# First batch of an attention and mixture-of-experts kernel: z's first group, v's maxima, constant matmuls and routing constants put elsewhere

## The chip, the cores and the metric

The kernel runs on one core of one Trainium2 chip. The metric is the device time of one execution in microseconds (us). TensorE, VectorE, ScalarE, GpSimd and SyncE are written PE, DVE, ACT, POOL and SP, as in the profile's rows. All DMAs of interest are issued on SP's queue.

## The reference

```
u, v: (8, 3072, 256)   z: (8, 3072, 64)   S = 3072
attn = max(z z^T / S, 0) ** 2
x    = (u * (attn v)).reshape(24576, 256)
logits = x w_gate ; expert = argmax(logits) ; gate = softmax(logits)[expert]
each of 8 experts takes its first 768 tokens, in order
out[token] = gate * relu(x w1[e]) w2[e] for kept tokens, 0 for the others
```

With 768 places for each of 8 experts, only the first tokens matter: the kernel computes attention for NB0 = 14 blocks of 512 query rows, checks on the chip that every expert is full, and runs the experts.

## The kernel before, in words

Every fp32 operand is split into two fp16 planes, "hi" and "lo", after a scaling by a power of two that comes from the largest absolute value (over partitions by an all-reduce on POOL). A block's attention runs over 12 pairs of key tiles of 128 (`attention`, line 723). For each pair PE makes the scores of both tiles (`sc`, line 772), ACT takes relu and square (lines 780, 784), DVE splits the square into hi and lo (`hl`, lines 788, 797), and PE multiplies with v's planes into four accumulators (`acc`, lines 872, 874: for each of 4 row tiles c and 2 key tiles one matmul of 512 columns and one of 256). Because attn is symmetric, strips of a block's squares are kept in DRAM (`kept`, line 809) and loaded turned by later blocks (`ld`, line 750). In block 1, pairs 0 and 1 come from such loads (pairs 12 and 13 of the whole sequence), and half of pair 15 comes from the core itself: line 803 sends two turning DMAs from `hl` into `corner`, and PE needs both at the first matmul of pair 15.

The first batch is prepared in `prepare(bt, True)` (line 315). z comes in three loads (line 337), then w_gate (`load_gate`, line 154), then v in six loads of 4 key tiles (line 343). Row norms of z (350, 354) give its maximum and, through POOL, its scale (`zb`). z is split and turned in six groups (`z_group`, line 375): hi on ACT (381), two DVE instructions (384, 385), eight transposes on PE into one PSUM tile `ztp` of one bank (392), and two copies out of it, one plane each, on ACT and DVE (395). Group 0 runs at once, the others when the planner's gates open. v's six maxima are dealt to ACT (loads 0, 2, 4, line 435) and DVE (loads 1, 3, 5, line 73), then reduced (442), all-reduced and turned into the scale (`v_bits`, `vs`); then v is split in pieces of two key tiles (456 on ACT, 459 on DVE). Thirty matmuls with an all-ones operand (`warm_up`, line 145) run on PE while z is loaded.

The order of the instructions on each engine is written by a planner (lines 170 to 272) that keeps its own clock for each engine (`clk`) with a cost for each item. Work is held in chains with a rank; `weave` goes through them by rank and emits what fits. A chain can wait for a gate (a key in `done`). Its clocks are costs that stand in the code and no times of the chip; they decide the order alone. A DMA with rank above 0 is emitted only while the DMA clock is at most 1.2 ahead of PE's (`fits`, line 244); DMAs of rank 0 and less, and loads, go past that rule. `need` moves PE's clock on until a key is there. Costs on the DMA clock: 1.46 for a `keep` or the load of u, 1.8 for a load of a kept strip, 2.3 for one of the eight writes that initialise `disp` (line 289), 4.4 for the next batch's z (`zraw`).

`more_consts` and `prep_gate` (lines 134, 156) make what the routing needs. They are a chain of rank 4, due at 25.0. `init_disp` (line 277), made at pair 1 with the gate "consts", clears a tile `dinit` on POOL (283), marks it on DVE (286) and writes it out in eight DMAs. At the end of every block `need` asks for the keys of all eight writes (line 881) before the block's routing is set up.

Of the kernel before, what the change touches and what calls it, by code (L numbers as in the profile page):

```python
# [9 lines left out]
F32 = mybir.dt.float32  # L10
F16 = mybir.dt.float16
I32 = mybir.dt.int32
AF = mybir.ActivationFunctionType
ALU = mybir.AluOpType
AX = mybir.AxisListType
# [3 lines left out]
P = 128  # L19
BLK = 512  # L20
# [6 lines left out]
def attention_moe_kernel(ctx: ExitStack, tc: tile.TileContext, u, v, z, w_gate, w1, w2, out, cap):  # L27
# [28 lines left out]
    def ts(o, i, s1, op0, s2=None, op1=None):  # L56
        if op1 is None:
            nc.vector.tensor_scalar(out=o, in0=i, scalar1=s1, scalar2=None, op0=op0)
        else:
            nc.vector.tensor_scalar(out=o, in0=i, scalar1=s1, scalar2=s2, op0=op0, op1=op1)  # L60
# [11 lines left out]
    def absmax(o, i):  # L72
        nc.vector.tensor_reduce(out=o, in_=i, axis=AX.XY if len(i.shape) == 3 else AX.X, op=ALU.max,
                                apply_absolute_value=True)
# [69 lines left out]

    def warm_up(n):

        t = ps.tile([P, BLK], F32, tag="m", name="warm")
        for _ in range(n):
            nc.tensor.matmul(t, lhsT=ones, rhs=ones.unsqueeze(1).to_broadcast([P, BLK // P, P]), start=True, stop=True)

    wg = const.tile([P, DC, E], F32, name="wg")

    def load_gate():
        nc.sync.dma_start(out=wg, in_=w_gate.rearrange("(c p) e -> p c e", p=P))
# [25 lines left out]
    def op(eng, cost, dep=0.0):  # L180
        start = max(clk[eng], dep + HOP)
        if eng in ("SP", "XB"):
            start = max(clk["SP"], dep + HOP)
            clk["SP"] = start + (0.5 if eng == "SP" else max(1.2, 0.3 + cost))
            clk["DMA"] = max(clk["DMA"], start + 1.4) + cost
            return clk["DMA"] + 1.0
        clk[eng] = start + cost
        return clk[eng]
# [126 lines left out]
    def prepare(bt, first=False):  # L315
# [5 lines left out]
        else:  # L321
            zr = row(z, bt.b).rearrange("(t p) d -> p t d", p=P)
        w = JT // zparts
        sq = []
        bt.vraw = {}
        key = lambda *k: (bt.id,) + k

        def ld_z(i):
            def f():
                if i == 0:  # L330
                    bt.zraw = sb.tile([P, JT, DQ], F32, tag="zraw", name="zraw", bufs=1)
                    bt.vm = sm.tile([P, NV], F32, tag="vm", name="vm")
                    bt.n2 = sm.tile([P, JT], F32, tag="n2", name="n2")
                    bt.zz = sb.tile([P, 2, S], F16, tag="zz", name="zz")
                zt = bt.zraw.rearrange("p (t r) d -> p t (r d)", r=2) if first else bt.zraw
                k = zt.shape[1] // zparts
                nc.sync.dma_start(out=zt[:, i * k:(i + 1) * k], in_=zr[:, i * k:(i + 1) * k])
            return f

        def ld_v(i):  # L340
            def f():
                t = sb.tile([P, 4, D], F32, tag="raw", name="vraw", bufs=6)
                nc.sync.dma_start(out=t, in_=vr[:, 4 * i:4 * i + 4, :])  # L343
                bt.vraw[i] = t
            return f
# [29 lines left out]
        def z_group(g):  # L375
            sl = slice(4 * g, 4 * g + 4)
            st = Bag()

            def hi():
                st.zhl = sb.tile([P, 4, 3 * DQ], F16, tag="zhl", name="zhl", bufs=3)  # L380
                nc.scalar.activation(st.zhl[:, :, 0:DQ], bt.zraw[:, sl], AF.Copy, scale=bt.zs)

            def lo():
                nc.vector.tensor_copy(st.zhl[:, :, 2 * DQ:3 * DQ], st.zhl[:, :, 0:DQ])
                nc.vector.scalar_tensor_tensor(out=st.zhl[:, :, DQ:2 * DQ], in0=bt.zraw[:, sl], scalar=bt.zs,
                                               in1=st.zhl[:, :, 0:DQ], op0=ALU.mult, op1=ALU.subtract)

            def tr():
                st.tp = ps.tile([P, 2, 4, P], F16, tag="m", name="ztp")
                for k in range(4):  # L390
                    for r in range(2):
                        nc.tensor.transpose(st.tp[:, r, k, :], st.zhl[:, k, r * DQ:r * DQ + P], ident)

            def ev(r):
                return lambda: (nc.scalar.copy if r else nc.vector.tensor_copy)(  # L395
                    bt.zz[:, r, g * BLK:(g + 1) * BLK].rearrange("p (t q k) -> p t k q", t=2, k=2),
                    st.tp[:, r].rearrange("p (t k) q -> p t k q", k=2))

            return [[("ACT", 0.4, hi, None)], [("DVE", 0.53, lo, key("zl", g))], [("PE", 0.5, tr, None)],
                    [("ACT", 0.48, ev(1), key("ze", g)), ("DVE", 0.6, ev(0), key("z", g))]]  # L400

        ZW = 6
# [26 lines left out]
            return ("SP", 1.2, f, key("z", 0) if h else None)  # L429

        def v_abs(i):
            def f():
                if first and i % 2 == 0:
                    junk = sb.tile([P, 4, D], F32, tag="x", name="junk")
                    nc.scalar.activation(junk, bt.vraw[i], AF.Abs, accum_out=bt.vm[:, i:i + 1])
                else:
                    absmax(bt.vm[:, i:i + 1], bt.vraw[i])
            return ("ACT", 1.04, f, None) if first and i % 2 == 0 else ("DVE", 1.13, f, None)

        def v_red():  # L440
            bt.vmx = sm.tile([P, 1], F32, tag="vmx", name="vmx")
            nc.vector.tensor_reduce(out=bt.vmx, in_=bt.vm, axis=AX.X, op=ALU.max)

        def v_all():
            bt.vma = sm.tile([P, 1], F32, tag="vma", name="vma")
# [6 lines left out]
        def v_piece(t0, k):  # L452
            o, i, a = slice(t0, t0 + k), t0 // 4, t0 % 4

            def hi():
                nc.scalar.activation(bt.v2[:, o, 0, :], bt.vraw[i][:, a:a + k], AF.Copy, scale=bt.vs)

            def lo():
                nc.vector.scalar_tensor_tensor(out=bt.v2[:, o, 1, :], in0=bt.vraw[i][:, a:a + k], scalar=bt.vs,  # L459
                                               in1=bt.v2[:, o, 0, :], op0=ALU.mult, op1=ALU.subtract)  # L460
                for j in range(t0 + 2, t0 + k, 2):
                    done[key("v", j // 2)] = clk["DVE"]

            return [[("ACT", 0.19 + 0.21 * k, hi, None)], [("DVE", 0.06 + 0.285 * k, lo, key("v", t0 // 2))]]

        def factor():
            q = sm.tile([P, 1], F32, tag="cb0", name="cb0")
# [13 lines left out]

        if first:
            tz = [(ld_z(i)(), op("SP", 0.75))[1] for i in range(zparts)]
            load_gate()
            tv = [(ld_v(i)(), op("SP", 1.46))[1] for i in range(NV)]
        for i in range(zparts):
            st = [[("ACT", 1.4 / zparts, norm1(i), None)], [("DVE", 1.7 / zparts, norm2(i), key("n", i))]]
            if first:
                Chain(st, -3, tz[i])
            else:  # L490
                Chain([[("SP", 4.4, ld_z(i), None)]] + st, 1, slow=8.0)
        for i in range(NV):
            def mark(i=i):
                e, c, f, _ = v_abs(i)
                return e, c, f, key("m", i)
            if first:
                Chain([[mark()]], -2, tv[i], gate={1: key("zl", 0), 2: key("ze", 0), 3: key("z", 0)}.get(i))
            else:
                Chain([[("SP", 1.46, ld_v(i), None)], [mark()]], 2, slow=8.0)

# [12 lines left out]
        def v_rest():  # L513
            chain = [[("DVE", 0.1, v_red, None)], [("POOL", 0.4, v_all, None)], [("DVE", 0.6, v_bits, key("vs"))]]
            if first:
                def pieces():
                    for i in range(JT // 2):
                        Chain(v_piece(2 * i, 2), -2, done[key("vs")], gate=("pair", i - 2) if i > 1 else None)
                chain.append([("PE", 0.0, pieces, None)])
            else:  # L520
                chain += pipe([v_piece(t, 4) for t in range(0, JT, 4)])
            Chain(chain, -2 if first else 2, need_max("m", NV))

        def need_max(k, n):
            return max(done[key(k, i)] for i in range(n))


        watchers.append((lambda: all(key("n", i) in done for i in range(zparts)), z_rest))
        watchers.append((lambda: all(key("m", i) in done for i in range(NV)), v_rest))
        watchers.append((lambda: key("s") in done and key("v", 0) in done and "gate" in done,  # L530
                         lambda: Chain([[("DVE", 0.4, factor, key("f"))]], 3, max(done[key("v", 0)], done["gate"]))))
        bt.key = key
# [190 lines left out]
    def attention(blocks, hook):  # L723
# [31 lines left out]
        def loads_to(p):  # L755
            while loads and loads[0] <= p:
                load(loads.popleft())
# [65 lines left out]
        def scores_to(k):  # L823
            while ahead[0] < len(computed) and computed[ahead[0]] < k:
                scores(*divmod(computed[ahead[0]], 2))
                ahead[0] += 1
# [14 lines left out]
                  -2, clk["PE"])  # L841

        loads_to(1)
        scores_to(4)
        for p in range(NP):
            n, g = divmod(p, NPAIR)
            bt, ib, c0, cc = blocks[n]
# [244 lines left out]
    with tc.manual_schedule():  # L1092
# [12 lines left out]
        prepare(b0, True)  # L1105
        make_consts()
        warm_up(30)
        Chain([[("DVE", 1.2, more_consts, "consts")], [("DVE", 0.8, prep_gate, "gate")]], 4, 25.0)

        def put_zeros(i):  # L1110
            def f():
# [105 lines left out]
```

## Time and profile before

| | us |
|---|---|
| median of three runs (lowest, highest) | 807.35 (807.35, 810.51) |
| profiled execution, its own time | 808.55 |
| its span, first to last instruction | 806.7 |
| PE busy | 781.0 (97%) |
| DVE, ACT, POOL busy | 536.7, 434.3, 130.2 |

Numbers in the views are us from the span's start; a stretch is written 0:30. A row of a timeline gives start, length, engine, line, operation, what is written and read, a count, and in brackets the idle time before it with what ended it. "xN" on a row merges N neighbours. PEclk is the granted clock of PE as a share of full speed: 1.00 is 2.4 GHz and 0.50 is 1.2 GHz.

### The profile page before, as it was taken

Reading aid. Unit: us, or ns where it says so; the run is one execution under the profiler, and the core shown is the slowest. Engines: PE = TensorE matmul, PEld = TensorE weight load, DVE = VectorE, ACT = ScalarE, POOL = GpSimd, SP = SyncE. Lnnn points to the kernel's source line nnn. Section 1 sums busy time; section 2 is a strip of 40 time slices with the busy share of each in tenths; the row PEclk is TensorE's granted clock in tenths of the full one; section 3 lists DMA queues with packets and bytes.
Section 4 is the critical chain, followed back from the end, with each engine's and each line's share of the span. In section 5 each row is a group of like instructions: output and inputs, shape, how many; then the busy total and the mean of one; then the engine's idle time right before and its main releaser. Section 6 shows DMA issues by size and latency. Waiting matters only on the chain.

```text
span 806.7 us, 13434 instructions
## 1 busy us (share of the span) xinstructions
PE 781.0 (97%) x4964; PEld 460.7 (57%) x4964; DVE 536.7 (67%) x1186; ACT 434.3 (54%) x748; POOL 130.2 (16%) x123
## 2 busy tenths in 40 slices
PE   6999999999999999999999999999799999999996
PEld 2555555555655555555556655565566666666663
DVE  6886887863536889976454359888674675665741
ACT  5786746461405767763524148674564564554541
POOL 0000121110202010202112020203211313303202
PEclk8799999999999999999999999999999999999999
DMA  6399998969897996949597969972797847655001
GB/s 195 131 339 253 309 256 205 262 173 226 187 202 154 305 281 168 277 129 269 136 270 172 202 153 297 272 188 78 183 323 291 260 137 285 217 164 173 27 14 44
DMA packets 278736, 165.48 MB, mean 205 GB/s; under 512 B 218125, under 2 KB 244058, under 8 KB 278656
## 3 DMA queue, kind: packets, MB, share of 16 engines
q1 hardware_dynamic: 273760, 151.69, 71.3%
q0 software_dynamic: 4896, 12.79, 4.7%
q8 instruction: 42, 0.69, 0.4%
q14 instruction: 38, 0.31, 0.1%
HBM read 35.86 MB, written 77.75 MB: 141 GB/s over the span
## 4 chain that ended last, share of the span: by engine, by line
PE 87%; DMA 5%; DVE 3%; SPq 2%; ACT 2%; issue 1%; POOL 0%; POOLq 0%; ACTq 0%
PE acc L872 32%; PE acc L874 16%; PE hps L1012 14%; PE sc L772 10%; PE yps L1033 10%; PE yps L1034 5%; DMA ld<-kept 2%; DMA vraw<-in_v 1%; DMA fxt<-disp 1%; DMA zz<-zhl 1%; SPq L584 1%; DVE hh L998 1%; PE lg L591 0%; SPq L343 0%; ACT r L780 0%
## 5 line engine op out<-in xcount | busy, mean ns | idle before, releaser
L872 PE MATMUL acc<-v,hl 128*128 128x512 f16 x760 | 257.7, 381 | 2.9 <-DVE v L459 2.9
L874 PE MATMUL acc<-v,hl 128*128 128x256 f16 x760 | 208.2, 274 | 0.0
L780 ACT ACTIVATE r<-sc 128x512 f32<-128x512 f32 (+1 forms) x212 | 116.1, 551 | 140.3 <-PE sc L772 133.4
L872 PE MATMUL acc<-v,ld 128*128 128x512 f16 x488 | 162.4, 379 | 3.4 <-DMA ld<-kept 2.0
L874 PE MATMUL acc<-v,ld 128*128 128x256 f16 x488 | 133.0, 272 | 0.0
L1012 PE MATMUL hps<-fxt,wt 128*128 128x384 f16 (+2 forms) x816 | 127.2, 316 | 4.0 <-DVE hh L998 1.8
L1033 PE MATMUL yps<-wt,hh 128*128 128x512 f16 x384 | 125.5, 379 | 0.0
L872 PEld LDWEIGHTS <-hl 128*128 128x128 f16 x760 | 74.7, 98 | 88.4 <-issue 1.9
L772 PE MATMUL sc<-zz 128*128 128x512 f16 (+1 forms) x424 | 118.6, 364 | 3.6 <-DVE zz L395 2.3
L797 DVE TENSOR_TENSOR hl<-a,hl 128x1024 f16<-128x1024 f32 (+1 forms) x106 | 118.2, 1115 | 3.5
L84 POOL DMA_INDIRECT disp<-xr,slot x54 | 67.6, 1252 | 300.0 <-ACT a L784 147.7
L1012 PEld LDWEIGHTS <-wt 128*128 128x128 f16 x816 | 76.0, 98 | 54.1 <-issue 5.1
L1034 PE MATMUL yps<-wt,hh 128*128 128x256 f16 x384 | 104.7, 273 | 0.4 <-DVE hh L998 0.4
L788 DVE CAST hl<-a 128x1024 f16<-128x1024 f32 (+1 forms) x106 | 67.9, 640 | 54.9 <-ACT a L784 47.7
L784 ACT ACTIVATE a<-r 128x1024 f32<-128x1024 f32 (+1 forms) x106 | 102.6, 968 | 3.2
L998 DVE SCALAR_TENSOR_TENSOR hh<-hps,hh 128x384 f16<-128x384 f32 (+2 forms) x136 | 70.7, 530 | 39.2 <-ACT hh L997 38.8
L997 ACT ACTIVATE hh<-hps 128x384 f16<-128x384 f32 (+2 forms) x136 | 62.9, 471 | 49.6 <-PE hps L1012 49.0
L874 PEld LDWEIGHTS <-hl 128*128 128x128 f16 x760 | 74.7, 98 | 24.2 <-issue 2.2
L872 PEld LDWEIGHTS <-ld 128*128 128x128 f16 x488 | 47.7, 98 | 56.9 <-DMA ld<-kept 3.3
L84 POOL DMA_INDIRECT out<-ys,sid x48 | 55.2, 1150 | 124.3 <-DVE ys L1043 86.1
L1033 PEld LDWEIGHTS <-hh 128*128 128x128 f16 x384 | 37.5, 98 | 44.1
L1040 ACT ACTIVATE ys<-yps,sg 128x256 f32<-128x256 f32 x48 | 22.8, 475 | 74.1 <-PE yps L1034 67.1
(134 smaller groups left out, 685.1 us busy)
## 6 DMA issues: line engine op xcount, KB each, us to landing
kept<-hl SPq DMA_DIRECT2D x62, 512.0 KB
out<-zero SPq DMA_DIRECT2D x48, 512.0 KB
wraw<-in_moe_w SPq DMA_DIRECT2D x32, 512.0 KB
vraw<-in_v SPq DMA_DIRECT2D x18, 512.0 KB
u<-in_u SPq DMA_DIRECT2D x13, 512.0 KB
disp<-dinit SPq DMA_DIRECT2D x8, 792.0 KB
zraw<-in_z SPq DMA_DIRECT2D x2, 768.0 KB
zz<-zz SPq DMA_DIRECT2D x4, 384.0 KB
```

The lines of the kernel that those rows point to most:

```text
L84: r = nc.gpsimd.indirect_dma_start(out=dst, out_offset=bass.IndirectOffsetOnAxis(ap=idx, axis=0), in_=src, in_offset=None, bounds_check=bo ...
L772: nc.tensor.matmul(s[:, 0:w], lhsT=bt.zz[:, 0, j * P:(j + 1) * P], rhs=bt.zz[:, r, q0:q0 + w], start=(r == 0), stop=(r == 1))
L780: nc.scalar.activation(sct[p][:, jj, :], s[:, 0:w], AF.Relu)
L784: nc.scalar.activation(sq[p], sct.pop(p), AF.Square)
L788: nc.vector.tensor_copy(hl[:, :, :, 0, :], sq[p].rearrange("p j (t k) -> p j t k", k=HB))
L797: nc.vector.tensor_sub(hl[:, :, :, 1, :], a.rearrange("p j (t k) -> p j t k", k=HB), hl[:, :, :, 0, :])
L872: nc.tensor.matmul(o, lhsT=a(0, jj, c), rhs=bt.v2[:, j], start=(j == 0), stop=False, skip_group_check=True)
L874: nc.tensor.matmul(o[:, 0, :], lhsT=a(1, jj, c), rhs=bt.v2[:, j, 0, :], start=False, stop=(j == JT - 1), skip_group_check=True)
L998: [("DVE", 0.07 + w * 0.00104, lambda: nc.vector.scalar_tensor_tensor(out=tl, in0=src, scalar=0.0, in1=th, op0=ALU.max, op1=ALU.subtract), ...
L1012: nc.tensor.matmul(o, lhsT=wx.w1[:, d, wp, f * P:(f + 1) * P], rhs=sx.xt[:, xp * DC + d, a:a + w], start=(q == 0), stop=(q == len(seq) - 1))
L1033: nc.tensor.matmul(y, lhsT=hid(0, f)[:, sl], rhs=w, start=(f == 0), stop=False, skip_group_check=True)
L1034: nc.tensor.matmul(y[:, 0], lhsT=hid(1, f)[:, sl], rhs=w[:, 0], start=False, stop=(f == FC - 1), skip_group_check=True)
```

## The change

In the first batch: w_gate is loaded behind v. z's group 0 takes its hi plane on DVE, and all groups' transposes go into two PSUM tiles, one for each plane. v's maxima become seven: load 5 is split into halves, and ACT takes loads 0 and 2 and the second half of 5, DVE takes 1, 3, 4 and the first half of 5. `warm_up` charges PE's planner clock for each matmul, takes its tile from `acc`, and is called in five more places: 5 matmuls behind group 0's transposes, 9 behind those of groups 1 and 2, 5 behind the scores of the first pair and 10 behind those of the second. v's first piece is split into its two key tiles, of rank -3. The chain with `more_consts` and `prep_gate` is due at 45.0.

```diff
     def warm_up(n):
-        t = ps.tile([P, BLK], F32, tag="m", name="warm")
+        t = ps.tile([P, BLK], F32, tag="acc", name="warm", bufs=4)
         for _ in range(n):
+            op("PE", 0.2155)
             nc.tensor.matmul(t, lhsT=ones, ...)
...
+        NM = NV + 1 if first else NV
...
             def hi():                                   # z_group
...
+                if g == 0:
+                    ts(st.zhl[:, :, 0:DQ], bt.zraw[:, sl], bt.zs, ALU.mult)
+                else:
+                    nc.scalar.activation(st.zhl[:, :, 0:DQ], bt.zraw[:, sl], AF.Copy, scale=bt.zs)
...
             def tr():
-                st.tp = ps.tile([P, 2, 4, P], F16, tag="m", name="ztp")
-                for k in range(4):
-                    for r in range(2):
-                        nc.tensor.transpose(st.tp[:, r, k, :], st.zhl[:, k, r * DQ:r * DQ + P], ident)
+                st.tp = [ps.tile([P, 4, P], F16, tag="m", name="ztp") for r in range(2)]
+                for r in range(2):
+                    for k in range(4):
+                        nc.tensor.transpose(st.tp[r][:, k, :], st.zhl[:, k, r * DQ:r * DQ + P], ident)
+                warm_up({0: 5, 1: 9, 2: 9}.get(g, 0))
...
-            return [[("ACT", 0.4, hi, None)], [("DVE", 0.53, lo, key("zl", g))], ...
+            return [[("ACT", 0.4, hi, None) if g else ("DVE", 0.3, hi, None)], [("DVE", 0.53, lo, key("zl", g))], ...
...
         def v_abs(i):
+            act = first and i in (0, 2, NV)
+            src = lambda: bt.vraw[min(i, NV - 1)][:, 2 * (i == NV):4 - 2 * (first and i == NV - 1)]
...
+            half = 0.5 if first and i >= NV - 1 else 1.0
+            return ("ACT", 1.04 * half, f, None) if act else ("DVE", 1.13 * half, f, None)
...
         if first:
             tz = [(ld_z(i)(), op("SP", 0.75))[1] for i in range(zparts)]
-            load_gate()
             tv = [(ld_v(i)(), op("SP", 1.46))[1] for i in range(NV)]
+            load_gate()
...
                 def pieces():
-                    for i in range(JT // 2):
+                    for t in (0, 1):
+                        Chain(v_piece(t, 1), -3, done[key("vs")])
+                    for i in range(1, JT // 2):
                         Chain(v_piece(2 * i, 2), -2, done[key("vs")], gate=("pair", i - 2) if i > 1 else None)
...
         loads_to(1)
+        scores_to(2)
+        if straight[0] and len(blocks) > 1:
+            warm_up(5)
         scores_to(4)
+        if straight[0] and len(blocks) > 1:
+            warm_up(10)
...
-        Chain([[("DVE", 1.2, more_consts, "consts")], [("DVE", 0.8, prep_gate, "gate")]], 4, 25.0)
+        Chain([[("DVE", 1.2, more_consts, "consts")], [("DVE", 0.8, prep_gate, "gate")]], 4, 45.0)
```

## Rows read from the trace of the kernel before

**Rows 1.** The page's busy times and instruction counts, PE, PEld, DVE, ACT and POOL with their shares of the span.
```profile
PE   781.0 (97%) x4964; PEld 460.7 (57%) x4964; DVE 536.7 (67%) x1186; ACT 434.3 (54%) x748; POOL 130.2 (16%) x123
```

**Rows 2.** The longest of PE's waits over the whole span: the instruction, whom it waited for, us in total, times, the longest.
```profile
PE acc L872 <- DVE v L459: 2.9, 1, 2.9
```

**Rows 3.** The windows view: for each stretch the busy time of PE, PEld, DVE, ACT and POOL with instruction counts, then PEclk, the DMA engines' share, GB/s.
```profile
12.00:13.00 1.00, 0.00 (x0) 0.00 (x0) 0.69 (x1) 1.00 (x2) 0.00 (x0) 0.88 1.11 351
...
29.50:30.00 0.50, 0.50 (x3) 0.29 (x2) 0.46 (x3) 0.50 (x2) 0.04 (x1) 0.67 0.17 33
```

**Rows 4.** The timeline of PE from 10 to 31.
```profile
10.91 0.61 PE L392 MATMUL ztp<-ident,zhl 128*128 128x128 f16 x8 [0.80 <-DVE zhl L385]
13.10 1.89 PE L772 MATMUL sc<-zz 128*128 128x512 f16 x4 [1.58 <-DVE zz L395]
...
21.00 0.59 PE L872 MATMUL acc<-v,hl 128*128 128x512 f16 x1 [2.87 <-DVE v L459]
...
26.15 1.89 PE L772 MATMUL sc<-zz 128*128 128x512 f16 x4 [0.73 <-DVE zz L395]
...
30.12 1.03 PE L772 MATMUL sc<-zz 128*128 128x512 f16 x4
```

**Rows 5.** The timeline of DVE from 12 to 30.
```profile
12.31 0.73 DVE L395 COPY zz<-ztp 128x512 f16<-128x512 f16 x1 [0.42 <-ACT zz L395]
...
15.85 1.22 DVE L73 TENSOR_REDUCE vm<-vraw 128x1 f32<-128x1024 f32 x1 [1.60 <-DMA vraw<-in_v]
17.18 0.16 DVE L442 TENSOR_REDUCE vmx<-vm 128x1 f32<-128x6 f32 x1
...
18.28 0.68 DVE L788 CAST hl<-a 128x1024 f16<-128x1024 f32 x1
19.00 1.23 DVE L797 TENSOR_TENSOR hl<-a,hl 128x1024 f16<-128x1024 f32 x1
20.19 2.07 DVE L459 SCALAR_TENSOR_TENSOR v<-vraw,vsr,v 128x512 f16<-128x512 f32 x3
...
26.84 0.27 DVE L58 TENSOR_SCALAR tri<-iota,part 128x128 f16<-128x128 f32 x1
...
28.78 0.78 DVE L58 TENSOR_SCALAR wg<-wg,wgsr 128x16 f16<-128x16 f32 x1
```

**Rows 6.** The timeline of ACT, z's group 0.
```profile
9.62 0.49 ACT L381 ACTIVATE zhl<-zraw,zb 128x256 f16<-128x256 f32 x1
```

**Rows 7.** The timeline of POOL.
```profile
17.44 0.36 POOL L77 PARTITION_ALL_REDUCE vma<-vmx  x1 [8.35 <-DVE vmx L442]
27.84 0.35 POOL L77 PARTITION_ALL_REDUCE wgma<-wgm  x1 [10.04 <-DVE wgm L73]
28.05 1.48 POOL L283 MEMSET dinit<- 128x1584 f32 x1
```

**Rows 8.** The windows view again (columns as in rows 3), while z, w_gate and v are loaded.
```profile
4.00:5.00 1.00, 1.00 (x4) 0.41 (x3) 0.48 (x1) 0.81 (x2) 0.00 (x0) 1.00 0.98 196
5.00:6.00 1.00, 1.00 (x4) 0.34 (x3) 0.87 (x2) 0.30 (x1) 0.00 (x0) 1.00 0.57 168
```

**Rows 9.** Groups of instructions from 0 to 31: line, engine, operation, out<-in, shapes, count, then busy us and mean ns of one, then idle time before them.
```profile
L354 DVE TENSOR_REDUCE n<-sq 128x8 f32<-128x512 f32 x3 | 2.1, 686 | 2.8 <-ACT sq L350 2.7
...
L385 DVE SCALAR_TENSOR_TENSOR zhl<-zraw,zb,zhl 128x256 f16<-128x256 f32 x3 | 1.4, 477 | 0.0
...
L58 DVE TENSOR_SCALAR ident<-iota,part 128x128 f16<-128x128 f32 x1 | 0.3, 286 | 0.0
```

**Rows 10.** The timeline of SP's DMA issues: the first of the eight writes of `disp`, and from the last `keep` of block 0 to the corner.
```profile
31.92 0.36 SPq L289 DMA_DIRECT2D disp<-dinit  x1
...
63.99 0.37 SPq L809 DMA_DIRECT2D kept<-hl  x1
64.42 1.62 SPq L289 DMA_DIRECT2D disp<-dinit  x2
66.14 1.15 SPq L337 DMA_DIRECT2D zraw<-in_z  x1
74.56 3.31 SPq L803 DMA_TRANSPOSE corner<-hl  x2
```

**Rows 11.** The page's DMA issues: out<-in, queue, operation, count, KB of each.
```profile
disp<-dinit SPq DMA_DIRECT2D x8, 792.0 KB
```

**Rows 12.** The DMA view of the stretches 68:70 and 72:74: packets, MB, mean rate, and how many packets were small.
```profile
DMA packets 128, 0.71 MB, mean 355 GB/s; under 512 B 16, under 2 KB 16, under 8 KB 128
...
DMA packets 2014, 0.52 MB, mean 258 GB/s; under 512 B 2014, under 2 KB 2014, under 8 KB 2014
```

**Rows 13.** The windows view (columns as in rows 3) around the corner's DMAs.
```profile
54.00:62.00 8.00, 8.00 (x48) 4.57 (x47) 5.53 (x7) 6.78 (x9) 0.00 (x0) 1.00 1.05 274
...
66.00:70.00 4.00, 4.00 (x25) 2.24 (x24) 2.33 (x6) 3.09 (x7) 0.00 (x0) 1.00 1.06 385
...
71.50:75.00 3.50, 3.50 (x23) 2.12 (x22) 3.33 (x11) 2.15 (x5) 0.00 (x0) 1.00 1.18 224
75.00:75.80 0.80, 0.80 (x6) 0.39 (x5) 0.76 (x2) 0.80 (x3) 0.00 (x0) 1.00 0.13 28
...
77.80:78.60 0.80, 0.80 (x6) 0.49 (x5) 0.77 (x2) 0.45 (x1) 0.00 (x0) 1.00 0.81 164
```

**Rows 14.** The timeline of PE, the corner's first use.
```profile
78.72 0.38 PE L872 MATMUL acc<-v,corner 128*128 128x512 f16 x1
```

More of the change, by code (lines that the diff above doesn't have):

```diff
@@ L331, in f @@
                     bt.zraw = sb.tile([P, JT, DQ], F32, tag="zraw", name="zraw", bufs=1)
-                    bt.vm = sm.tile([P, NV], F32, tag="vm", name="vm")
+                    bt.vm = sm.tile([P, NV + 1], F32, tag="vm", name="vm")
                     bt.n2 = sm.tile([P, JT], F32, tag="n2", name="n2")
@@ L380, in hi @@
                 st.zhl = sb.tile([P, 4, 3 * DQ], F16, tag="zhl", name="zhl", bufs=3)
-                nc.scalar.activation(st.zhl[:, :, 0:DQ], bt.zraw[:, sl], AF.Copy, scale=bt.zs)
+                if g == 0:
+                    ts(st.zhl[:, :, 0:DQ], bt.zraw[:, sl], bt.zs, ALU.mult)
+                else:
+                    nc.scalar.activation(st.zhl[:, :, 0:DQ], bt.zraw[:, sl], AF.Copy, scale=bt.zs)
             def lo():
@@ L396, in ev @@
                     bt.zz[:, r, g * BLK:(g + 1) * BLK].rearrange("p (t q k) -> p t k q", t=2, k=2),
-                    st.tp[:, r].rearrange("p (t k) q -> p t k q", k=2))
-            return [[("ACT", 0.4, hi, None)], [("DVE", 0.53, lo, key("zl", g))], [("PE", 0.5, tr, None)],
+                    st.tp[r].rearrange("p (t k) q -> p t k q", k=2))
+            return [[("ACT", 0.4, hi, None) if g else ("DVE", 0.3, hi, None)], [("DVE", 0.53, lo, key("zl", g))], [("PE", 0.5, tr, None)],
                     [("ACT", 0.48, ev(1), key("ze", g)), ("DVE", 0.6, ev(0), key("z", g))]]
@@ L431, in v_abs @@
         def v_abs(i):
+            act = first and i in (0, 2, NV)
+            src = lambda: bt.vraw[min(i, NV - 1)][:, 2 * (i == NV):4 - 2 * (first and i == NV - 1)]
             def f():
-                if first and i % 2 == 0:
+                if act:
                     junk = sb.tile([P, 4, D], F32, tag="x", name="junk")
-                    nc.scalar.activation(junk, bt.vraw[i], AF.Abs, accum_out=bt.vm[:, i:i + 1])
-                else:
-                    absmax(bt.vm[:, i:i + 1], bt.vraw[i])
-            return ("ACT", 1.04, f, None) if first and i % 2 == 0 else ("DVE", 1.13, f, None)
+                    n = src().shape[1]
+                    nc.scalar.activation(junk[:, 0:n], src(), AF.Abs, accum_out=bt.vm[:, i:i + 1])
+                else:
+                    absmax(bt.vm[:, i:i + 1], src())
+            half = 0.5 if first and i >= NV - 1 else 1.0
+            return ("ACT", 1.04 * half, f, None) if act else ("DVE", 1.13 * half, f, None)
         def v_red():
             bt.vmx = sm.tile([P, 1], F32, tag="vmx", name="vmx")
-            nc.vector.tensor_reduce(out=bt.vmx, in_=bt.vm, axis=AX.X, op=ALU.max)
+            nc.vector.tensor_reduce(out=bt.vmx, in_=bt.vm[:, 0:NM], axis=AX.X, op=ALU.max)
         def v_all():
@@ L462, in lo @@
                     done[key("v", j // 2)] = clk["DVE"]
-            return [[("ACT", 0.19 + 0.21 * k, hi, None)], [("DVE", 0.06 + 0.285 * k, lo, key("v", t0 // 2))]]
+            return [[("ACT", 0.19 + 0.21 * k, hi, None)], [("DVE", 0.06 + 0.285 * k, lo, key("v", t0 // 2) if t0 + k > t0 // 2 * 2 + 1 else None)]]
         def factor():
@@ L483, in prepare @@
             tz = [(ld_z(i)(), op("SP", 0.75))[1] for i in range(zparts)]
+            tv = [(ld_v(i)(), op("SP", 1.46))[1] for i in range(NV)]
             load_gate()
-            tv = [(ld_v(i)(), op("SP", 1.46))[1] for i in range(NV)]
         for i in range(zparts):
@@ L491, in prepare @@
                 Chain([[("SP", 4.4, ld_z(i), None)]] + st, 1, slow=8.0)
-        for i in range(NV):
+        for i in range(NM):
             def mark(i=i):
@@ L496, in prepare @@
             if first:
-                Chain([[mark()]], -2, tv[i], gate={1: key("zl", 0), 2: key("ze", 0), 3: key("z", 0)}.get(i))
+                Chain([[mark()]], -2, tv[min(i, NV - 1)], gate={1: key("zl", 0), 2: key("ze", 0), 3: key("z", 0)}.get(i))
             else:
@@ L521, in v_rest @@
                 chain += pipe([v_piece(t, 4) for t in range(0, JT, 4)])
-            Chain(chain, -2 if first else 2, need_max("m", NV))
+            Chain(chain, -2 if first else 2, need_max("m", NM))
         def need_max(k, n):
@@ L528, in prepare @@
         watchers.append((lambda: all(key("n", i) in done for i in range(zparts)), z_rest))
-        watchers.append((lambda: all(key("m", i) in done for i in range(NV)), v_rest))
+        watchers.append((lambda: all(key("m", i) in done for i in range(NM)), v_rest))
         watchers.append((lambda: key("s") in done and key("v", 0) in done and "gate" in done,
```

## The prediction

> **What bounds the kernel now.** I read the page's busy times first: PE is busy for 781.0 of 806.7 us [rows 1], so a change in one stage is worth what it moves PE there. PE's waits come next: the longest one of all is the first `acc` matmul, which waits 2.9 us for v's first piece [rows 2]. From 30 us on PE hardly pauses, so the first batch's preparation costs its own length, and a later stall of PE costs its own length too. Third come the timelines of PE and DVE between 10 and 31: the reader is to see three gaps on PE, before the first scores at 13.10, before the first `acc` at 21.00 and before the scores at 26.15, and the next pair's scores at 30.12 [rows 4]. I use 30.12 as the mark for the front: everything of pair 0 is done there. The windows view shows the clock: it falls to 1.2 GHz within 12:13, after the warm-up matmuls end at 10.1 and eight transposes and a gap follow, and comes back to 2.4 GHz within 29.5:30, after PE has worked without a gap from 26.15 [rows 3, 4]. Last I follow SP's queue to the end of block 0, because the change moves eight large DMAs on it [rows 10].
>
> A measurement of this kernel tells about 0.5% (4 us) from no change.
>
> **The front, part by part.**
>
> *w_gate behind v.* Its small packets hold up the DMA engines: 196 and 168 GB/s in 4:5 and 5:6, against 351 later [rows 3, 8]. That is (155 + 183)/351, about 1.0 us of DMA time. Between 0 and 1.0 I take 0.9: the last of v lands at 14.95 in place of 15.85 [rows 5].
>
> *z's group 0.* On DVE hi costs between 0.29 (half as long a row, from fp32 to fp16 with a pointer) and the 0.49 that ACT takes [rows 6, 9]; the hop between engines goes. With two banks DVE's copy doesn't wait for ACT's: it started at 12.31, 0.42 late and 0.73 long [rows 5]. So scores start about 1 us before 13.10. I cost all this at nothing for the end: v's maximum is late behind it (15.85). Were v no longer late, this 1 us would count.
>
> *v's maxima.* Load 5's DVE half takes 0.69 in place of 1.22 [rows 5, 9]; ACT's half lies beside it. Without anything else the reduction `vmx` would move from 17.18 to about 15.7.
>
> *The order turns round.* The planner's clock now counts the warm-up matmuls: 30 bring PE to 6.67, the transposes and 5 more to 11.34, two scores, 5, two scores and 10 to 16.30, where pair 0 opens the gate of z's group 2. In that pass its hi and lo end at 15.75 on the planner's clocks; transposes are allowed 0.5 later, at 16.25, so they just fit, and its evictions follow. v's reduction chain is made only when a pass begins, so `vmx` comes behind group 2's two DVE instructions and its eviction. Before, group 2's DVE work stood behind v's first pieces. On the chip: both halves end at 15.65; ACT's hi 0.49 more, 16.15; from there to the transposes took 0.80 in group 0, 16.95; transposes 0.61, eviction 0.73, so `vmx` is at 18.3, 1.1 later than now [rows 4 to 6]. In the queue behind it are the scale, the first square's split and all of v's pieces.
>
> *The constants go, the clearing of `dinit` comes.* DVE loses 26.84 to about 29.8 [rows 5]; PE has none of these waits, so it gains nothing by itself. But `init_disp`'s clearing on POOL needs nothing from DVE. Emitted now before the gate's all-reduce, it stands right behind v's all-reduce. Before, it ended 1.69 after the start of the all-reduce in front of it [rows 7]; now that is 18.3 + 0.26 + 1.69 = 20.3. The row that shows a price: the gate's fp32-to-fp16 scaling of 16 elements took 0.78 beside that clearing and ended with it, where one of 128 elements took 0.29 alone [rows 5, 7, 9]. The first cast of `hl` would start 1.10 behind `vmx`, at 19.4 [rows 5]; between 0 and 0.9 I take 0.9, so 20.3. The Trainium skill (SBUF — State Buffer, section Who interferes with whom) speaks against the change here: a DVE cast or scaling in a two-port mode and a GpSimd instruction hold a shared pair of ports exclusively, and the later one blocks fully. By that rule the whole 0.9 is paid; without it the sum is 0.9 less. The trace has the one row that agrees.
>
> *First `acc`.* From cast to v's piece 1.91, a piece of one tile 0.48 [rows 5, 9]: 22.7, against 21.00, 1.7 later.
>
> *Warm-ups and pair 0.* The 38 new matmuls at 0.2155 cost nothing where PE waits. They hold the clock to about 19.6, when the nine behind group 2's transposes end. Then PE waits 3.1 us, longer than the 2.7 after which the clock fell within 12:13, so I take it as fallen again [rows 3, 4]. In exchange group 2 is done, and the gap before 26.15 shrinks. From 22.7: eight half-speed matmul pairs to 25.4, group 1's transposes, nine fillers, four scores, eight pairs: 30.5 if the clock comes back 3.7 us after 22.7 as it did after 26.15, 31.9 if later, 29.9 if it never fell. Against 30.12 I take **+0.6**, bounds -1.2 (no blocking, clock held) and +2.3.
>
> **The corner.** Constants due at 45 instead of 25 delay all eight writes of `disp`; the first is planned at 47.6 instead of 29. On the planner's DMA clock a write (2.3) goes only when that clock is within 1.2 of PE's; keeps, u and two strip loads go past it and fill it. Following the clocks pair by pair, write 0 goes in pair 5, write 1 at the end of pair 7, and then none until the last keep. The other six come out together, because block 0's end needs their keys. On SP they stand behind the last keep (63.99) and ahead of `zraw` and the corner's two turning DMAs. Now two stand there [rows 10].
>
> The queue is in order: `zraw` was issued at 66.14 to 67.29, yet its small packets are not in 68:70 (16) but in 72:74 (2014) [rows 10, 12]. The engines were full in 54:62 and until 75.0, then empty; the corner's second transfer ended at 78.6, and PE used it at 78.72 with no slack seen [rows 13, 14]. A write is 792 KB at 385 GB/s, 2.1 us [rows 11, 13]. Four more put the end of `zraw` at 75.0 + 8.4 = 83.4. The two transposes then follow at once, since SP issued them meanwhile: 0.8 each [rows 13], 85.0. PE comes in step with the front, so its shift cancels: at most 85.0 - 78.6 = 6.4. Idle time of the engines within 54 to 75 may swallow some. Bounds 3 and 8 (transposes as slow as now: 3.6 from 75.0 to 78.6), I take **+5.5**. A PE idle so long loses its clock by the same row: 3.7 us at half speed [rows 3, 4], between 0 and 1.8, I take **+1.8**. Nothing behind gives it back: PE is the bound.
>
> *Costed at nothing:* v's first piece in two halves (ACT half a tile ahead of DVE); the seventh column of `vm`; `warm`'s bank; the 2.6 us of constants put into DVE near 48, covered by squares prepared three pairs ahead (without that cover up to 2.6).
>
> **Sum.** 0.6 + 5.5 + 1.8 = 7.9. On the profiled execution's 808.55 that is 816.45; it stands 1.2 above the median, so against 807.35 I predict **815.2**.
>
> **Rivals.**
> 1. *Not slower: the corner is in time.* If no more than two or three writes are left behind the last keep, or the engines had 5 us to spare, the queue ends near 77 and only the front counts: 807.35 + 0.6, about 808.0, from 806.1 to 809.7. For it: DMA is nearly free until 46. Against it: 54:62 is full [rows 13], and 78.6 to 78.72 leaves no slack. Deciding point: `zraw`'s packets end by 76. Chance 0.25.
> 2. *The corner's transposes take their 3.6 us after the queue has run dry, and the clock comes back late:* 8 + 1.8 + 2.3, 819.4. Chance 0.13.
> 3. *The front pays fully:* the clock holds from the warm-ups through pair 0, `vmx` near 15.7 because group 2 does not stand ahead of it, first `acc` near 19.5, pair 0 done at 26: -4.1, 803.2 with the corner in time. Against it is the order above. Chance 0.06.
> The forecast has 0.56, its own range 811 to 818.
>
> **How the numbers follow.** Slower by over 0.5%: forecast and rival 2, less a part that stays within 4 us, 0.65. Same: rival 1 and that part, 0.28. Faster: 0.07. The range 805.8 to 818.6 leaves out most of rival 3 and of rival 2.
>
> **What would show it.** On DVE `vmx` behind a copy of `zz`; a cast of `hl` that starts as `dinit`'s clearing ends; first `acc` at 22 to 23; two writes of `disp` ahead of block 0's last keep and six behind; a wait of PE on corner of 3 to 8 us near 78 with PEclk at 0.50 after it. If the writes stand otherwise, or PE doesn't wait there, the corner step is wrong; if `vmx` comes before 17, the order step is.

## The result and the profile after

The changed kernel takes 819.22 us (median; 817.51 to 821.08), the kernel before 807.85 beside it: ratio 1.0133, 95% interval 1.0107 to 1.0159. The forecast was 815.2, so the direction was right; the time lies 0.6 above the top of the range. The kernel before was 0.5 slower here than the 807.35 that the forecast started from: the ratio on 807.35 gives 818.1, just inside the range. In run 1 below, one of twelve executions took 1180.17 at a granted clock of 0.654; it counts in that run's median (808.24; 808.06 without it) and not in its ratio. The profiled execution took 819.1, with a span of 817.3 against 806.7: 10.6 us to explain, where the forecast had 7.9. One profile stands for one execution: the one of the kernel before took 808.55, 0.7 above its median.

Counting the 128x512 `acc` matmuls from the start in both timelines of PE, and comparing the starts of the same ones, gives a ledger of where PE falls behind:

| the n-th such matmul | before | after | behind | what lies between |
|---|---|---|---|---|
| 8th, end of pair 0 | 29.76 | 30.01 | 0.25 | the front |
| 105th | 71.79 | 75.50 | 3.71 | a wait for `relu` |
| 111th | 74.17 | 79.47 | 5.30 | half clock |
| 118th | 77.31 | 84.15 | 6.84 | logits, now ahead of it, and a wait for `xt` |
| 121st, first of the corner | 78.72 | 89.16 | 10.44 | a wait for the corner |
| 127th | 81.10 | 93.16 | 12.06 | half clock |
| 334th | 166.93 | 176.65 | 9.72 | part given back |

PE's waits of the changed kernel between 60 and 110 (us in total, times, longest). Before, the only one there was 1.3 for a drain.
```profile
PE acc L891 <- DMA corner<-hl: 3.4, 1, 3.4
PE sc L786 <- ACT r L794: 3.3, 1, 3.3
PE lg L605 <- DMA xt<-xr: 0.9, 1, 0.9
```
The windows view of the changed kernel (columns as in rows 3): two stretches at 1.2 GHz, each just after one of the long waits.
```profile
72.00:75.00 3.00, 0.00 (x0) 0.00 (x0) 2.15 (x11) 2.07 (x5) 0.00 (x0) 1.00 1.02 414
76.00:79.40 3.40, 3.40 (x12) 1.55 (x11) 2.95 (x4) 2.20 (x5) 0.00 (x0) 0.53 0.98 371
84.00:90.00 6.00, 2.52 (x17) 1.30 (x18) 3.62 (x10) 1.65 (x2) 0.00 (x0) 0.99 1.00 183
90.20:93.40 3.20, 3.20 (x11) 1.50 (x10) 0.00 (x0) 0.71 (x2) 0.00 (x0) 0.52 0.94 318
```
SP's queue after, to set beside [rows 10]. Two writes of `disp`, the last keeps, six writes, as forecast; but then `xt` and `zraw` go ahead of the corner, where before it was `zraw`, corner, `xt`.
```profile
48.81 0.34 SPq L290 DMA_DIRECT2D disp<-dinit  x1
...
54.38 0.46 SPq L290 DMA_DIRECT2D disp<-dinit  x1
...
63.31 1.30 SPq L823 DMA_DIRECT2D kept<-hl  x2
64.66 7.24 SPq L290 DMA_DIRECT2D disp<-dinit  x6
74.46 8.23 SPq L598 DMA_TRANSPOSE xt<-xr  x4
82.75 0.58 SPq L339 DMA_DIRECT2D zraw<-in_z  x1
83.42 4.80 SPq L817 DMA_TRANSPOSE corner<-hl  x2
```
ACT's timeline there. `relu` (L794), for which PE waits from 71.98 to 75.28, could have run at 69.2, when its scores were done, but stands behind the routing's casts (L587), and those wait for a chain of DVE.
```profile
68.76 0.37 ACT L853 COPY x<-acc 128x256 f32<-128x256 f32 x1 [0.28 <-PE acc L893]
72.69 0.91 ACT L587 ACTIVATE xr<-x,rsr 128x256 f16<-128x256 f32 x2 [3.56 <-DVE rsr L60]
73.84 0.91 ACT L587 ACTIVATE xr<-x,rsr 128x256 f16<-128x256 f32 x2 [0.24 <-DVE xr L653]
74.65 0.57 ACT L794 ACTIVATE r<-sc 128x512 f32<-128x512 f32 x1
```
Both inversions have one cause in the code, and runs 3 and 9 show it: putting PE's planned clock back takes both away, and moving that clock alone brings both. Line 900 asks for the keys of all eight writes (`need`), and `need` moves the planner's PE clock on by 0.1 until they are there. Followed through the planner's costs, that wait is 1.4 us before and 9.3 after (67.1 to 76.4), since the writes that are left pass one by one at 2.3 each. When it is over, the routing of block 0 seems long due and the next scores only just made, so the routing is put first on ACT and SP.

The front, to set beside [rows 4, 5, 7]: PE, then DVE, then POOL.
```profile
12.53 1.04 PE L786 MATMUL sc<-zz 128*128 128x512 f16 x4 [0.88 <-DVE zz L401]
...
18.72 2.10 PE L150 MATMUL warm<-ones 128*128 128x512 f16 x9
23.52 0.39 PE L891 MATMUL acc<-v,hl 128*128 128x512 f16 x1 [2.70 <-DVE v L471]
...
30.34 1.03 PE L786 MATMUL sc<-zz 128*128 128x512 f16 x4
```
```profile
18.69 0.73 DVE L401 COPY zz<-ztp 128x512 f16<-128x512 f16 x1 [0.57 <-PE ztp L397]
19.32 0.14 DVE L454 TENSOR_REDUCE vmx<-vm 128x1 f32<-128x7 f32 x1
...
20.39 1.42 DVE L802 CAST hl<-a 128x1024 f16<-128x1024 f32 x1
21.84 1.23 DVE L811 TENSOR_TENSOR hl<-a,hl 128x1024 f16<-128x1024 f32 x1
```
```profile
19.55 0.36 POOL L77 PARTITION_ALL_REDUCE vma<-vmx  x1 [11.14 <-DVE vmx L454]
19.78 1.49 POOL L284 MEMSET dinit<- 128x1584 f32 x1
```
The reduction `vmx` stands behind group 2's copy, the cast beside the clearing takes 1.42 instead of 0.68, and the first `acc` is 2.5 late; but it runs at full clock (0.39), and pair 0 ends 0.2 late.

### The profile page after: what moved, and what is told of

Its sections match the earlier page's. It is cut to its first block, busy times and chain, and to the rows that moved or that the text cites. A ratio compares the mean times of both kernels' runs of the same rounds, so it can differ in the third digit from the quotient of the medians.

```text
span 817.3 us, 13505 instructions
## 1 busy us (share of the span) xinstructions
PE 786.6 (96%) x5002; PEld 462.9 (57%) x5002; DVE 538.5 (66%) x1189; ACT 433.5 (53%) x748; POOL 129.1 (16%) x123
## 4 chain that ended last, share of the span: by engine, by line
PE 84%; DMA 7%; DVE 5%; ACT 2%; SPq 1%; issue 1%; POOL 0%; POOLq 0%; DVEq 0%; ACTq 0%
PE acc L891 30%; PE acc L893 15%; PE hps L1031 14%; PE yps L1052 10%; PE sc L786 9%; PE yps L1053 5%; DMA ld<-kept 2%; DMA vraw<-in_v 1%; DMA fxt<-disp 1%; DMA corner<-hl 1%; DVE hl L802 1%; DMA zz<-zhl 1%; DMA kept<-hl 1%; SPq L345 1%; DVE hh L1017 1%
## 5 line engine op out<-in xcount | busy, mean ns | idle before, releaser
L794 ACT ACTIVATE r<-sc 128x512 f32<-128x512 f32 (+1 forms) x212 | 115.6, 551 | 146.5 <-PE sc L786 137.9
L1059 ACT ACTIVATE ys<-yps,sg 128x256 f32<-128x256 f32 x48 | 22.7, 474 | 74.8 <-PE yps L1053 67.8
```

What stands on the lines that cost most here:

```text
L794: nc.scalar.activation(sct[p][:, jj, :], s[:, 0:w], AF.Relu)
```

## The experiments

All times are medians; "of before" is the ratio to the kernel before with its 95% interval. In what follows, order means that ACT's and SP's queues are turned round at block 0's end, and transfers the six late writes themselves. The table in the expectations is `disp`. "On kernel 1" means that the edit was made to the kernel of run 1; the others are edits of the changed kernel, where nothing else is said.

**1. The constants early again.**
```
-... prep_gate, "gate")]], 4, 45.0)
+... prep_gate, "gate")]], 4, 25.0)
```


> The changed kernel with the routing constants due at 25.0 again; its front stays as changed. Theory A (the late constants make the whole loss: at the end of block 0 the planner has to wait for the table's writes and puts everything behind them out of order): the PE waits of 3.3 (score matmul behind relu) and 3.4 (corner) and the two stretches at 1.2 GHz go, about 10.5 us of the 10.6; span within 1.5 us of before, time 806 to 809. The cast of the first weights takes 0.68 again, since the table's clearing on POOL is again behind the all-reduce of w_gate, and the first acc comes at 22.8 instead of 23.52. Theory B (the new front, its warm-ups and its other order are a good part of the loss later on): 811 or more. Theory C (my forecast's split: corner 5.5, clock 1.8, front 0.6): 808.5.

808.24, 1.0008 of before (0.9991 to 1.0025). All of the loss goes with this one number, and what is left of the change is worth nothing that can be measured. Behind the last keeps, SP's queue is the old one:
```profile
63.74 1.87 SPq L290 DMA_DIRECT2D disp<-dinit  x2
65.72 1.21 SPq L339 DMA_DIRECT2D zraw<-in_z  x1
73.89 2.50 SPq L817 DMA_TRANSPOSE corner<-hl  x2
76.50 5.13 SPq L598 DMA_TRANSPOSE xt<-xr  x4
```
The cast takes 0.68 again, the first `acc` comes at 22.39.

**2. The constants late, nothing else.** The kernel before, with 25.0 changed to 45.0.

> The kernel before with the constants due at 45.0 and nothing else. Theory A: the planner's wait at the end of block 0 grows from 1.4 to 10.6 on its own clock, and both PE stalls and both falls of the clock appear as in the changed kernel: plus 10 to 12 us, 818 to 820. Theory B: about half of it, 812 to 814. Theory C (only the transfers ahead of the corner count): plus 7.3, 815.

817.52, 1.0108 of before (1.0073 to 1.0144); by the ratio 8.7 us, less than the 10 to 12 of theory A. The same two waits of PE are there:
```profile
75.63 0.58 PE L772 MATMUL sc<-zz 128*128 128x256 f16 x2 [3.30 <-ACT r L780]
...
90.30 0.39 PE L872 MATMUL acc<-v,corner 128*128 128x512 f16 x1 [2.10 <-DMA corner<-hl]
```
The clock falls behind the first alone (0.61 in 76:79, 1.00 in 90:94). Theory B falls with runs 1 and 2.

**3. PE's planned clock put back.**
```
+ pe = clk["PE"]
  need(bt.key("f"), *[("init", e) for e in range(E)])
+ clk["PE"] = pe
```


> The changed kernel with constants due at 45.0; at the end of block 0 the eight writes are asked for as before and stand at the same place in SP's queue, but the planner's PE clock is put back afterwards to what it was, so that what follows isn't held to be 9.3 us late. Theory A (order): relu is no longer behind the routing's casts on ACT (the PE wait of 3.3 and its 1.6 of slow clock go), the corner's two turning DMAs go ahead of xt's four and of zraw: they are issued about 73 instead of 83.4, PE waits 0 to 1 for the corner; 808 to 811. Theory C (transfers): the six writes of 7.2 us are still ahead of the corner, which PE waits for as I forecast, 5.5 and 1.8 for the clock: 815.

820.71, 1.0164 (1.0120 to 1.0207): no gain, neither theory's number. At the corner it does half of what A said: no wait for `relu`, and the corner goes ahead of `xt`, at 72.87; but the corner is waited for 2.9, where A had 0 to 1, and the clock falls behind it (0.62 in 82:85.5). PE is 4.6 behind at the 127th `acc` instead of 12.06. But the planner's clocks of SP and DMA stayed moved, `zraw` went out at 88.88 instead of 82.75, and the next batch's work came into block 1's end. There ACT waits for a buffer that SP's transposes free late, `relu` behind it, and PE for that:
```profile
126.70 0.61 ACT L416 ACTIVATE zhl<-zraw,zb 128x384 f16<-128x384 f32 x1 [6.99 <-DMA zz<-zhl]
```
```profile
128.73 1.01 PE L786 MATMUL sc<-zz 128*128 128x512 f16 x2 [5.76 <-ACT r L794]
```

**4. v's reduction ahead of group 2** (on kernel 1).
```
-... gate=("pair", max(2 * g - 5, 0)) if g > 1 else key("vs"))
+... gate=("pair", 2 * g - 5) if g > 2 else key("vs"))
- warm_up({0: 5, 1: 9, 2: 9}.get(g, 0))    + warm_up({0: 5}.get(g, 0))
- warm_up(10)   + warm_up(20)              - op("PE", 0.2155)
```


> The kernel of the first run of this group (constants due at 25.0) with v's reduction ahead of z's group 2: groups 1 and 2 start with v's scale known, the fillers behind groups 1 and 2 go, the fillers behind the first scores are 5 and 20 instead of 5 and 10, and the planner is charged nothing for fillers. If the copy of group 2 ahead of the reduction sets the first acc (19.32 against 17.1 for the last maximum), the first acc comes near 20.5 to 21, at 2.4 GHz, the end of pair 0 near 27 instead of 30.3, and the time is 803 to 805.5. If it is the landing of v or the clock, no earlier than the first run of this group: 807 to 808.5.

807.55, 1.0000 (0.9984 to 1.0016). The first `acc` comes at 19.67, earlier than expected and at full clock, but the 5th only at 27.00: in PE's queue the transposes and scores of group 1 come first, and now they are what is late (four scores take 1.83, at half clock, instead of 1.03). The 803 to 805.5 expected for an early first `acc` was missed.

**5. All the planner's clocks put back**: `was = dict(clk)` ahead of `need`, `clk.update(was)` behind it.

> As the kernel with the PE clock put back (the third of the group before), but all of the planner's clocks are put back after the eight writes were asked for, SP's and the DMA's too. Its plan then puts, behind the six writes, zraw, the corner's two DMAs and xt's four, which is the order my forecast worked with. Theory A' (the late writes cost twice: by the planner's moved clock, and by their own transfers ahead of the corner; the 9 us that the run before lost at block 1's end came from zraw behind xt, at 88.9): relu waits on nothing new, PE waits for the corner alone, 3 to 6, and 1.5 for the clock, nothing at block 1's end: plus 4 to 7, 811 to 814. Theory C (transfers alone): the forecast's 7.3, 814 to 815. Theory A (order alone): no more than 809.

816.2, 1.0119 (1.0089 to 1.0149). That is more than any of the three theories said. This is the order that my forecast assumed, and its price: one wait of 6.1 for the corner, then 2.8 at half clock (PE is 9.1 behind at the 129th `acc`), nothing at block 1's end.
```profile
64.49 8.02 SPq L290 DMA_DIRECT2D disp<-dinit  x6
72.61 1.20 SPq L339 DMA_DIRECT2D zraw<-in_z  x1
73.91 10.23 SPq L817 DMA_TRANSPOSE corner<-hl  x2
```
```profile
85.08 0.61 PE L891 MATMUL acc<-v,corner 128*128 128x512 f16 x1 [6.12 <-DMA corner<-hl]
```

**6. The constants due at 35.0.**

> The changed kernel with the constants due at 35.0. By its plan three writes instead of six are asked for at the end of block 0, and the planner's PE clock is moved by 6.0 instead of 9.3. That is still beyond the next scores, so relu stands behind the routing's casts and the corner behind xt as before. Theory A' : the stall of 3.3 behind relu with its 1.6 of slow clock stays whole, the corner is waited for 1 to 3 less: plus 5 to 9, 813 to 817. Theory C (what counts is the number of transfers ahead of the corner): three writes of 1.2 on SP less, plus 3 to 4, 811. If the loss went with the planner's wait itself, two thirds of 10.5: plus 7, 815.

811.3, 1.0063 (1.0040 to 1.0086). That is theory C's number, but not its way: the wait for `relu` is whole (3.30), the corner, issued at 78.56 with `zraw` behind it, isn't waited for, and the clock does not fall behind the wait (1.00 in 74.2:78). By 78.56 the four writes are past, and the time is that of run 9, which has much the same order without them; so they cost nothing that shows, and the order still does.
```profile
63.54 5.32 SPq L290 DMA_DIRECT2D disp<-dinit  x4
73.34 5.12 SPq L598 DMA_TRANSPOSE xt<-xr  x4
78.56 2.53 SPq L817 DMA_TRANSPOSE corner<-hl  x2
```

**7. No fillers** (on kernel 1): the `warm_up` calls behind groups and scores taken out.

> The changed kernel with constants due at 25.0 and none of the fillers: no matmuls of constants behind z's groups and behind the first scores. If they are what holds TensorE's clock up in the front, the first acc take 0.75 instead of 0.39 and the windows from 12 to 30 show a clock of 0.5 to 0.9, as before; the end of pair 0 is then at 29.5 to 31 although the planner, charged nothing, puts v's reduction ahead of group 2: 807 to 809. If the clock stays up without them, the end of pair 0 is at 27 to 28 and the time 804 to 806.

806.97, 1.0001 (0.9986 to 1.0016). Without the fillers the clock is 0.50, and the first two `acc` of 512 columns take 0.58 and 0.63 (0.39 for the first in run 1).
```profile
20.00:22.00 2.00, 1.36 (x5) 0.68 (x5) 1.87 (x5) 2.00 (x5) 0.00 (x0) 0.50 0.00 0
```
It costs nothing all the same: v's reduction (16.90) is no longer behind group 2, and the first `acc` comes at 20.64 instead of 22.39.

**8. Group 1 early** (on kernel 4): group 1 gated by `key("z", 0)`, group 2 by `key("v", 0)`, constants due at 22.0.

> The version that the runs so far point to: constants due at 22.0, z's group 1 started right behind group 0, group 2 behind v's first piece, v's reduction ahead of both, fillers only behind group 0 and the first scores, the planner charged nothing for them. If the wait for group 1's scores behind the first acc (19.67 to 27.0 in the run with v first) is what gave the front's gain back, the end of pair 0 comes at 24 to 26 instead of 30.1 and the time is 802 to 804.5. If what is gained in front is lost again at block 0's end, where PE then meets loads and tables that come no earlier, the time is 806 to 808.

806.33, 0.9988 (0.9969 to 1.0007). Pair 0's last `acc` is 5.0 earlier than before, but at pair 2 half of that is gone: from 24.7 to 29.7 DVE does mostly constants ahead of its cast (30.19), and PE waits.
```profile
30.93 0.39 PE L890 MATMUL acc<-v,hl 128*128 128x512 f16 x1 [1.24 <-DVE hl L801]
...
32.19 0.28 PE L892 MATMUL acc<-v,hl 128*128 128x256 f16 x1 [0.87 <-DVE hl L810]
```

**9. The order without the writes** (kernel 1, `clk["PE"] += 8.0` behind `need` in block 0).

> The changed kernel with the constants due at 25.0, so that the writes go as early as before (one is left for the end of block 0), but the planner's PE clock is moved on by 8.0 at the end of block 0 by hand. That gives the orders of the changed kernel (relu behind the routing's casts on ACT, xt and zraw ahead of the corner on SP) without its six late writes. With the runs so far this is the fourth corner of a square: neither (808.2), late writes without the order (816.2), both (819.2), and here the order without the writes. If the order is a cost of its own: the PE wait of 3.3 behind relu, with or without 1.6 of slow clock behind it, and up to 1 for the corner, which is turned behind xt, 811 to 814. If the order costs only because the transfers are slow: 807 to 809.

812.19, 1.0072 (1.0044 to 1.0099). This was the number expected if the order is a cost of its own. Order alone costs about 5.8 us against before: the wait for `relu`, then two for `xt`, since its logits now come at 78.14 and its last DMA is issued till 79.53.
```profile
75.22 0.38 PE L786 MATMUL sc<-zz 128*128 128x256 f16 x2 [3.30 <-ACT r L794]
...
78.14 0.35 PE L605 MATMUL lg<-wg,xt 128*128 128x16 f16 x8
...
79.50 0.26 PE L605 MATMUL lg<-wg,xt 128*128 128x16 f16 x4 [1.01 <-DMA xt<-xr]
...
80.86 0.26 PE L605 MATMUL lg<-wg,xt 128*128 128x16 f16 x4 [1.11 <-DMA xt<-xr]
...
85.82 0.39 PE L891 MATMUL acc<-v,corner 128*128 128x512 f16 x1 [0.36 <-DMA corner<-hl]
```

**10. Only what nobody needs early is late** (on kernel 8).
```
+ Chain([[("DVE", 0.5, slot_consts, "consts")]], 4, 22.0)     # tslot, maximum of w_gate
+ Chain([[("DVE", 0.9, more_consts, None)], [("DVE", 1.6, prep_gate, "gate")]], 4, 45.0)
- Chain([[("DVE", 1.2, more_consts, "consts")], [("DVE", 0.8, prep_gate, "gate")]], 4, 22.0)
- ("POOL", 1.0, fill, None)   + ("POOL", 1.6, fill, None)     # and clk put back as in 5
```


> The eighth kernel's front, with the routing constants in two parts: what the table's writes need (two small operations) and the maximum of w_gate stay early (due 22.0), the rest of the constants and the scaling of w_gate are due at 45.0 as in the change; the clearing is taken to last longer by the planner, so that the table's stamp isn't asked for too early; the planner's clocks are put back after the writes were asked for. In the eighth run 4 us of constants stood on DVE between 24.7 and 29.7 ahead of pair 2's cast, and PE waited 1.2 and 0.9 for it. If that is what gave back half of the front's gain, the lead over before at pair 4 is 4.5 to 5 instead of 2.5, and the time is 803 to 805.5. If the lead is lost at the loads of block 0's end or later whatever it is: 805.5 to 807.5.

804.49, 0.9975 (0.9962 to 0.9988): faster than both kernels. The interval leaves out no change, though 2.0 us is less than the 4 that the prediction said a measurement can tell. In the profile the lead over before is 4.8 at pair 4, 4.0 at the 334th `acc` and still 4.0 at the 1000th of 1296, but 2.6 at the 1200th; by the ratio about 2.0 of it is left in the time. Run 1 too moves by 1.3 against before between the 334th and the last, so one profile of each doesn't show where the rest goes.

## Why the forecast held, and where it failed

Runs 1, 5 and 9 and the changed kernel make a square:

| ratio to before | old order | turned order |
|---|---|---|
| writes early | 1.0008 (run 1) | 1.0072 (run 9) |
| six writes late | 1.0119 (run 5) | 1.0133 (changed) |

Against run 1 the order alone costs 0.0064, 5.2 us, the transfers alone 0.0111, 9.0 us, and both together 0.0125, 10.1 us: each is a cost by itself, and together they cost some 4 us less than their sum (between 0 and 8, if the four intervals are combined). The transfers are both time on SP's queue and time of the DMA engines, and no run parts these. A reason for the smaller sum is in the traces: while PE waits for `relu` the transfers run on, and the wait for the corner is 3.4 instead of 6.1.

**The corner step: the right place, one of two causes.** The writes stand as I worked out, two ahead of the last keep and six behind, and they are transfers that the corner waits for: in the order I assumed it is 6.1 (run 5) against my 5.5. What I left out is in the same sentence of the prediction, "block 0's end needs their keys": I followed what that does to SP, not that the planner's PE clock stands in that `need` for 9.3 us and so turns round every queue behind it. My order on SP was the old one behind the six writes; the real one had `xt` and `zraw` ahead of the corner, and on ACT the casts ahead of `relu`.

**The clock behind the stall:** the size for one was near, 1.8 against 1.6, but there were two stalls and two falls, 3.2. With 3.5 around `relu`, 1.5 at the logits and 3.6 at the corner, PE falls 11.8 behind from the 8th `acc` to the 127th; some 1.5 comes back later. Of the 11.8 the step that I named makes 5.2 (3.6 and 1.6, against 5.5 and 1.8), and what I had put at nothing makes 6.6: the wait for `relu`, its clock and the logits. So it is partly luck that the total lies within about 4 us of the forecast: one stall stands in for a part of the other.

**The front, +0.6 against +0.2: right by errors that cancel.**
- *w_gate behind v, 0.9 earlier:* wrong. The last load's maximum starts at 15.85 and 15.78 in the two profiles with w_gate ahead (before, run 2), and between 15.23 and 16.53, mean 15.7, in the ten with it behind (the changed kernel and runs 1, 3 to 10). The small packets lower the rate where they pass [rows 8], but without them v lands 0.1 earlier on the mean, less than it moves from profile to profile, and in none at the 14.95 that I took.
- *The order of `vmx`:* right, though 1.0 later than my 18.3, and with it the first `acc` is at 23.52 instead of 22.7. It is at 19.32 behind group 2's copy, and at 16.07 in run 4, where that stands behind it.
- *The clearing beside the cast:* right in size. The cast took 1.42 in five kernels with the clearing behind v's all-reduce (the changed one, runs 2, 3, 5, 6) and 0.68 in six without (runs 1, 4, 7 to 10): 0.74 against my 0.9. By the Trainium skill (SBUF — State Buffer, section Who interferes with whom) the later one blocks fully. The trace agrees in the length: the cast's record begins at its time, 20.39, not late, but its end goes with the clearing's, 0.54 behind it in the changed kernel and 0.54 or 0.55 in runs 2, 3, 5 and 6. Run 10 shows it once more: there the clearing (25.35 to 26.84) meets the third cast, which takes 1.68 and ends 0.54 behind it too.
```profile
25.70 1.68 DVE L805 CAST hl<-a 128x1024 f16<-128x1024 f32 x1
```
- *The clock in the gap before the first `acc`:* wrong. PE waited 2.70 and the clock stayed up (1.00 in 20:24), which gave back what the later `acc` had lost. Run 7, without fillers, has 0.50 there, but so much is not sure with them: run 5 has the same front and 0.81.

**The rivals.** "The corner is in time" is refuted by the waits of PE. "3.6 us after the queue has run dry" is nearest to the time, but by another way: there was a second wait, for `relu`, and its clock. "The front pays fully" was not to be had, even where the first `acc` came early (run 4).

## What to carry to other kernels

Where a planner orders queues by its own clocks, a step that is made later costs not only its transfers: follow what the planner's clock does while it waits for that step, and which work seems due when the wait is over. When two causes make one stall, taking away one of them may show nothing (run 3 did) or move the stall; make all four combinations before naming one. And delay only what nobody is waiting for: of some 4 us of constants, the 0.5 on which eight large writes hung had to stay early.

## What the runs showed of the hardware

- Transposing DMAs behind a full queue are issued slowly too: `xt`'s four took 8.23 us on SP's queue behind six writes and 5.13 in runs 1 and 9; the corner's two 10.23 in run 5, behind the six writes and `zraw`, 4.61 in run 9, right behind `zraw` alone, and 2.50 in run 1.
- The same wait of 3.30 for `relu` was followed by the lower clock in the changed kernel (0.53 in 76.0:79.4) and in run 2 (0.61 in 76:79), and not in runs 6 and 9 (1.00 in 74.2:78 and in 76:79). Likewise the first `acc` waited 2.7 in the changed kernel and in run 5, which has the same front: there the clock was 0.81 in 20:24, here 1.00. What decides stays open.
- The start of the front moves from profile to profile with the same code: z's scale came at 9.12 before and at 8.35 in run 2, so a shift of less than a microsecond there says nothing.
